# An RWKV layer with two mixtures behind it: operands laid out by the host instead of transposed on TensorE

## The chip, the cores and the metric

The kernel runs on one core of a Trainium2 chip. The metric is the device time of one execution in microseconds; lower is better. The time before is the median of three runs.

## The reference, cut to what matters

Three stages follow one another. The first is a linear attention with a state of 48 x 48 per head (4 batches, 8 heads, 768 tokens, head dimension 48); the second multiplies two projections and sends the product through `w3` and `w_out`; the third is a mixture of eight experts, weighted by a gate that is normalised eight times over rows and columns.

```python
for t in range(S):                                   # r, k, v, w: (4, 8, 768, 48)
    cur = np.einsum('bhd,bhe->bhde', u[None] * kt, vt)
    y[:, :, t] = np.einsum('bhd,bhde->bhe', rt, state + cur)
    state = wt[:, :, :, None] * state + np.einsum('bhd,bhe->bhde', kt, vt)
x = y.transpose(0, 2, 1, 3).reshape(3072, 384)
x = (((x @ w1) * (x @ w2)) @ w3) @ w_out             # 384 -> 1024 -> 1024 -> 384
P = gate(x @ w_gate)                                 # exp, then 8 row and column normalisations
out = sum(P[:, e:e+1] * (np.maximum(x @ W1[e], 0) @ W2[e]) for e in range(8))
```

The four weights of the second stage come as float64, all other inputs as float32.

## The kernel before, in words

The order of the instructions is written out by hand (line 73), and each engine's queue works in that order. The program has two parts.

The first part runs over slices `s` (loop at line 721). Attention works on 24 units of 128 tokens, four slices a unit: in its first slice a unit's successor is prepared (`stage_a0`, `stage_a1`), and then come `stage_b`, `stage_c1` and `stage_c2` for the unit itself. From slice 15 on, each slice also holds one step of the second stage of the reference for a block of 384 tokens (three units): eight steps of `moe_a` and `moe_b` (tiles `pa`, `pb`, `gs`), then four of `moe_x2` (`po`). W3 times W_out is multiplied out once beforehand, strip by strip, in slices 3 to 14 (`w34_mm`, tile `w34ps`, eight accumulating matmuls a strip), so that `moe_x2` needs one product in place of two.

In `stage_a0` and `stage_a1` (lines 273 to 357) PE transposes w, k and r of a unit, four 128 x 128 matmuls against the identity each (tiles `trw`, `trk`, `trr`), since the loads put tokens on partitions and the scans need the head dimension there. ACT copies `trw` into `w33`, where each 32 tokens have a 33rd column of zero that restarts a scan. DVE scans `w33` forwards and backwards (`Ft`, `Gt`) and multiplies `trk` and `trr` by them (`f_ks`, line 320; `f_rp`, line 332), out of PSUM. These steps are put off in a queue `aux`, from which two are taken in each slice and the rest in the last slice of a unit. GpSimd multiplies r and k with tokens on partitions (`f_rk`, line 304).

Weights in float64 are loaded as pairs of 32-bit words into tiles `raw` (line 155, three buffers), and converted by an ACT instruction (`conv1`) and three integer instructions of DVE (`conv2`). There are twenty conversions: four pieces of `w_out` (`o`), eight strips of W3 (`3`), eight strips of W1 and W2 (`i`). Their places among the slices are the lists at lines 24 to 26; each conversion issues the load for the one four places behind it (`next_load`, line 561). Each strip of W3 is transposed on PE in eight matmuls (`w34_tr`, line 232), whose result ACT copies to `w3th` for `w34_mm`.

All DMAs of the kernel are issued by SP, in program order. A load of r, k, w or v has 1024 runs of 48 numbers. The loads of unit n + 3 for w, k and r are issued in the second slice of unit n (line 758).

The second part (line 1026 on) is the experts: tiles `zp` and `yp`, with weights split into a high and a low half by ACT, POOL and DVE, and x kept in device memory and loaded again for each expert.

Of the kernel before, what the change touches and what calls it, by code (L numbers as in the profile page):

```python
# [31 lines left out]
def tile_rwkv_moe_sinkhorn_moe(
    ctx: ExitStack,
    tc: tile.TileContext,
    r: bass.AP,
    k: bass.AP,
# [117 lines left out]
    def raw_tile(n):  # L154
        return tmp.tile([P, n, 2], U32, tag="raw", bufs=3, name="raw")
# [34 lines left out]
    def load_w12(i):  # L190
        src = (moe_w1, moe_w2)[i % 2].bitcast(U32)
        c0 = 2 * FC * (i // 2)
        raw = raw_tile(KD * FC)
        rv = raw.rearrange("p (q c) t -> p q (c t)", q=KD)
        for hh in range(2):
            nc.sync.dma_start(rv[64 * hh:64 * hh + D],
                              src[0:2 * D * KD, c0:c0 + 2 * FC].rearrange(
                                  "(q h p) c -> h p q c", q=KD, h=2)[hh])
# [60 lines left out]

    w34_ops = [("t", 0, 0), ("t", 0, 1)] if W34_LEAD else []  # L260
    for s in range(NF):
        if s == W34_LEAD:
            w34_ops += [("t", s, 0), ("t", s, 1)]
        if W34_LEAD <= s < NF - 1:
            w34_ops += [("t", s + 1, 0), ("t", s + 1, 1)]
        w34_ops += [("m", s, g) for g in range(NF)]
        if s + 1 < W34_LEAD:
            w34_ops += [("t", s + 1, 0), ("t", s + 1, 1)]

    W33B = w33[:, 1:529].rearrange("p (b s) -> p b s", s=33)  # L270
# [190 lines left out]
    def moe_a(blk, f):  # L461
# [76 lines left out]
    tot = sum(0.45 if o_[0] == "t" else 0.645 for o_ in w34_ops)  # L538
    done = 0.0
    for o_ in w34_ops:  # L540
        w34_at.setdefault(W34_0 + int((done + 0.2) / tot * W34_N), []).append(o_)
# [537 lines left out]
```

## Time and profile before

| | us |
|---|---|
| median of 3 runs | 2096.4 |
| lowest and highest run | 2095.07, 2097.36 |
| profiled execution, span from first to last instruction | 2097.3 |
| PE busy | 2047.5 |
| DVE busy | 1136.3 |
| ACT busy | 551.8 |
| POOL busy | 483.4 |

The profile is of one execution and its span is its own time: 0.9 us above the median. Busy times of the engines overlap; the share of one of them in a stretch of the span tells which engine that stretch may hang on, and the waits and the chain of work that ended last tell what it does hang on.

### The profile page before, as it was taken

The numbers are of one execution on the slowest core, as the hardware profiler recorded it, in microseconds if no ns is written. First come the engines' busy times: TensorE is split into PE (matmuls) and PEld (weight loads), VectorE is DVE, ScalarE is ACT, GpSimd is POOL, SyncE is SP. The second block draws the span as 40 slices with busy tenths as digits, with TensorE's granted clock in tenths as the row PEclk, the third lists the DMA queues.
The fourth block names the chain that finished last, engine by engine and source line by source line (L and its number), as shares of the span: only waits on it lengthen the run. The fifth ranks groups of instructions, "written<-read, shape, count | busy, mean of one in ns | idle before, by whom it ended". The sixth has DMA issues, their size and how long they took to land.

```text
span 2097.3 us, 37994 instructions
## 1 busy us (share of the span) xinstructions
PE 2047.5 (98%) x16427; PEld 1992.6 (95%) x16427; DVE 1136.3 (54%) x1792; ACT 551.8 (26%) x956; POOL 483.4 (23%) x487
## 2 busy tenths in 40 slices
PE   5879999999999999999999999999999999999999
PEld 3569999999999999999999999999999999999999
DVE  8785666661575454454445444544545454445454
ACT  3443333333422221131223122211321131123111
POOL 4475555555513210030003001200300030011000
PEclk7999999999999999999999999999999999999999
DMA  8652222211412322132124122321321232213220
GB/s 241 135 102 42 50 50 50 50 21 48 181 46 91 113 84 91 72 119 97 46 91 151 46 91 77 120 91 46 136 105 47 91 116 81 91 61 117 102 84 31
DMA packets 145287, 183.67 MB, mean 88 GB/s; under 512 B 105120, under 2 KB 133856, under 8 KB 137952
## 3 DMA queue, kind: packets, MB, share of 16 engines
q1 hardware_dynamic: 145120, 181.25, 27.0%
q8 instruction: 129, 2.11, 0.4%
q14 instruction: 38, 0.31, 0.1%
HBM read 161.17 MB, written 18.87 MB: 86 GB/s over the span
## 4 chain that ended last, share of the span: by engine, by line
PE 93%; DVE 2%; DMA 2%; ACT 1%; POOL 1%; issue 0%; SPq 0%; DVEq 0%; ACTq 0%; POOLq 0%
PE yp L83 38%; PE zp L83 35%; PE po L83 5%; PE pa L83 5%; PE pb L83 4%; PE w34ps L83 2%; PE yt L83 1%; DMA raw<-in_moe_w_dram 1%; DMA raw<-in_moe_w_out_dram 1%; PE sc L83 1%; PE trn L83 1%; PE up L83 0%; PE trk L83 0%; PE trw L83 0%; PE trr L83 0%
## 5 line engine op out<-in xcount | busy, mean ns | idle before, releaser
L83 PE MATMUL zp<-xc,w1h 128*128 128x256 f32 x4224 | 782.2, 280 | 0.8 <-ACT t L868 0.8
L83 PEld LDWEIGHTS zp<-xc,w1h 128*128 128x128 f32 x4224 | 691.9, 189 | 2.0 <-ACT t L868 1.3
L83 PE MATMUL zp<-xc,w1l 128*128 128x256 f32 x2112 | 595.0, 282 | 0.0
L83 PE MATMUL yp<-w2h,hh 128*128 128x384 f32 x1536 | 518.3, 337 | 0.0
L83 PE MATMUL yp<-w2l,hh 128*128 128x384 f32 x1536 | 517.1, 337 | 0.7 <-DVE w2l L666 0.7
L83 PE MATMUL yp<-w2h,hl 128*128 128x384 f32 x1536 | 516.9, 337 | 0.0
L83 PEld LDWEIGHTS zp<-xc,w1l 128*128 128x128 f32 x2112 | 398.6, 189 | 0.0
L845 ACT ACTIVATE hh<-cc 128x512 fp32r<-128x512 f32 x288 | 182.2, 633 | 797.3 <-DVE cc L852 797.3
L652 POOL TENSOR_TENSOR w1l<-w1raw,w1h 128x768 fp32r<-128x768 f32 x32 | 59.2, 1848 | 1086.4 <-ACT w1h L651 1086.4
L83 PEld LDWEIGHTS yp<-w2h,hh 128*128 128x128 f32 x1536 | 290.0, 189 | 0.4 <-issue 0.2
L83 PEld LDWEIGHTS yp<-w2l,hh 128*128 128x128 f32 x1536 | 289.0, 188 | 0.9 <-DVE w2l L666 0.9
L83 PEld LDWEIGHTS yp<-w2h,hl 128*128 128x128 f32 x1536 | 288.5, 188 | 0.0
L852 DVE TENSOR_TENSOR cc<-u,zp 128x512 f32<-128x512 f32 x192 | 131.9, 687 | 269.1 <-PE zp L83 269.1
L852 DVE TENSOR_TENSOR u<-t,zp 128x512 f32<-128x512 f32 x192 | 132.0, 687 | 200.3 <-PE zp L83 164.6
L849 DVE SCALAR_TENSOR_TENSOR hl<-cc,hh 128x512 fp32r<-128x512 f32 x288 | 198.8, 691 | 7.2 <-ACT hh L845 7.1
L960 DVE SCALAR_TENSOR_TENSOR acc<-yp,Pm,acc 128x384 f32<-128x384 f32 x168 | 103.5, 616 | 116.6 <-PE yp L83 116.5
L845 ACT ACTIVATE hh<-zp 128x512 fp32r<-128x512 f32 x96 | 57.5, 599 | 257.1 <-PE zp L83 257.1
L849 DVE SCALAR_TENSOR_TENSOR hl<-zp,hh 128x512 fp32r<-128x512 f32 x96 | 65.9, 687 | 74.5 <-ACT hh L845 74.4
L490 POOL TENSOR_TENSOR gl<-gs,gh 128x384 fp32r<-128x384 f32 x64 | 71.4, 1116 | 110.6 <-ACT gh L489 110.5
L852 DVE TENSOR_TENSOR vv<-u,zp 128x512 f32<-128x512 f32 x96 | 66.0, 688 | 49.8 <-PE zp L83 49.7
L868 ACT ACTIVATE t<-zp 128x512 f32<-128x512 f32 x96 | 57.5, 598 | 131.9 <-PE zp L83 131.9
L488 DVE TENSOR_TENSOR gs<-pb,asb 128x384 f32<-128x384 f32 x64 | 35.6, 556 | 104.0 <-PE pb L83 65.8
(151 smaller groups left out, 2366.4 us busy)
## 6 DMA issues: line engine op xcount, KB each, us to landing
xc<-xd SPq DMA_DIRECT2D x42, 2304.0 KB, 8.7
xd<-xc SPq DMA_DIRECT2D x6, 2304.0 KB, 7.0
w2raw<-in_moe_w_dram SPq DMA_DIRECT2D x32, 384.0 KB, 3.4
raw<-in_moe_w_dram SPq DMA_DIRECT2D x8, 1024.0 KB, 5.9
w1raw<-in_moe_w_dram SPq DMA_DIRECT2D x32, 256.0 KB, 2.9
nat_w<-in_w_dram SPq DMA_DIRECT2D x24, 192.0 KB, 2.9
nat_k<-in_k_dram SPq DMA_DIRECT2D x24, 192.0 KB, 2.9
nat_r<-in_r_dram SPq DMA_DIRECT2D x24, 192.0 KB, 3.5
```

Of the source, the lines that this page charges most:

```text
L83: nc.tensor.matmul(o, lhsT, rhs, start=start, stop=stop, **kw)
L488: nc.vector.tensor_tensor(gs, pb, asb, op=ALU.mult)
L490: nc.gpsimd.tensor_tensor(gl[:, f, :], gs, gh[:, f, :].bitcast(F32), op=ALU.subtract)
L652: nc.gpsimd.tensor_tensor(lo[:, d0:d0 + n, :], src, hi[:, d0:d0 + n, :].bitcast(F32), op=ALU.subtract)
L845: nc.scalar.activation(hh, src, AF.Relu)
L849: nc.vector.scalar_tensor_tensor(hl, src, 0.0, hh.bitcast(F32), op0=ALU.max, op1=ALU.subtract)
L852: nc.vector.tensor_tensor(o, a, b_, op=ALU.add)
L868: nc.scalar.activation(t1, b1, AF.Copy)
L960: nc.vector.scalar_tensor_tensor(dst, ya[t], Pm[:, tt, e:e + 1], dst, op0=ALU.mult, op1=ALU.add)
```

## The change

The host lays the inputs out otherwise; it moves and copies numbers, and calculates nothing. The kernel then loads each tile as one contiguous run per partition.

- r and k come twice: with the head dimension on partitions (`rt`, `kt`, 128 x 512 per unit), and with tokens on partitions (`rn`, `kn`, 128 x 384) for GpSimd's product. w comes with the head dimension on partitions, the restarting zeros already in place (128 x 529). v comes padded to 64 columns a head. The tile `w33`, ACT's copy into it, the transposes of r, k, w and `stage_a1` go; DVE's scans and products read the loaded tiles.
- W3 comes with its two sides swapped within each strip, so that `w34_mm` reads the converted strip; `w34_tr` and the copies `w3th` go. The converted strips have three buffers of their own.
- `raw` has two buffers, not three; the second piece of `w_out` is loaded into a tile that shares its place with the later halves of x (`xhl`, one tile in place of `xh` and `xl`).
- The PSUM buffers of the transposes go to the tag `moe`, four in place of two.
- The steps of `w34_mm` have places of their own (`W34_AT`), from slice 3 to 13.5.
- The loads of unit n + 3 are issued at the end of the last slice of unit n.
- W1, W2, W_out, the gate and the experts' weights are loaded by one DMA a tile.

```diff
-W34_0 = 3
-W34_N = 12
-W34_LEAD = 2
+W34_AT = (3, 4, 5.5, 6.5, 7.5, 9, 10.5, 12, 13.5)
...
+    SRC = {"r": (rt, NP * P), "k": (kt, NP * P), "v": (v, H * DP), "w": (w, 16 * 33 + 1),
+           "rn": (rn, H * D), "kn": (kn, H * D)}
     nat = {}
-    for nm in ("r", "k", "w", "v"):
+    for nm in SRC:
         for j in range(2):
-            nat[nm, j] = att.tile([P, H, DP], F32, name=f"nat_{nm}{j}")
-            nc.vector.memset(nat[nm, j][:, :, D:DP], 1.0 if nm == "w" else 0.0)
-    w33 = att.tile([P, 16 * 33 + 1], F32, name="w33")
-    nc.vector.memset(w33[:, 0:528].rearrange("p (b s) -> p b s", s=33)[:, :, 0:1], 0.0)
-    nc.vector.memset(w33[:, 528:529], 0.0)
+            nat[nm, j] = att.tile([P, SRC[nm][1]], F32, name=f"nat_{nm}{j}")
 
     def load(u_, nms):
-        b, t0 = u_ // UPB, (u_ % UPB) * P
         for nm in nms:
-            src = {"r": r, "k": k, "w": w, "v": v}[nm]
-            nc.sync.dma_start(nat[nm, u_ % 2][:, :, 0:D],
-                              src[b, :, t0:t0 + P, :].rearrange("h t d -> t h d"))
+            nc.sync.dma_start(nat[nm, u_ % 2], SRC[nm][0][u_])
...
-        return tmp.tile([P, n, 2], U32, tag="raw", bufs=3, name="raw")
+        return tmp.tile([P, n, 2], U32, tag="raw", bufs=2, name="raw")
...
-        if q == NF // 2 - 1:
-            raw = moe.tile([P, 2 * DM, 2], U32, tag="gl", name="wo_raw")
+        if q % 2:
+            raw = moe.tile([P, 2 * DM, 2], U32, tag=("xhl", "gl")[q // 2], name="wo_raw")
         else:
             raw = raw_tile(2 * DM)
-        nc.sync.dma_start(
-            raw.rearrange("p (a d) t -> p a (d t)", a=2),
-            moe_w_out[2 * q * P:2 * (q + 1) * P, :].bitcast(U32).rearrange("(a p) d -> p a d", p=P))
+        nc.sync.dma_start(raw.rearrange("p n t -> p (n t)"), moe_w_out[q].bitcast(U32))
...
     def load_w12(i):
-        src = (moe_w1, moe_w2)[i % 2].bitcast(U32)
-        c0 = 2 * FC * (i // 2)
         raw = raw_tile(KD * FC)
-        rv = raw.rearrange("p (q c) t -> p q (c t)", q=KD)
-        for hh in range(2):
-            nc.sync.dma_start(rv[64 * hh:64 * hh + D],
-                              src[0:2 * D * KD, c0:c0 + 2 * FC].rearrange(
-                                  "(q h p) c -> h p q c", q=KD, h=2)[hh])
-            x1 = D * (2 * KD + hh)
-            nc.sync.dma_start(rv[64 * hh + D:64 * hh + 64],
-                              src[x1:x1 + D, c0:c0 + 2 * FC].rearrange("(q p) c -> p q c", q=KD))
+        nc.sync.dma_start(raw.rearrange("p n t -> p (n t)"), (moe_w1, moe_w2)[i % 2][i // 2].bitcast(U32))
...
-        cvs["3", s] = conv1(raws["3", s], FF)
+        cvs["3", s] = conv1(raws["3", s], FF, tmp.tile([P, FF], F32, tag="w3c", bufs=3, name="w3c"))
...
-    def w34_tr(s, q):
-        raw = w3c[s]
-        if q == 0:
-            w3t[s] = tmp.tile([P, NF, P], F32, tag="w3t", bufs=2, name="w3th")
-        th = w3t[s]
-        pt = ps.tile([P, 4, P], F32, tag="moe", bufs=2, name="w3pt")
-        for j in range(4):
-            g = 4 * q + j
-            mm(pt[:, j, :], raw[:, g * P:(g + 1) * P], ident, True, True, tr=True)
-        nc.scalar.activation(th[:, 4 * q:4 * q + 4, :], pt, AF.Copy)
-        if q == 1:
-            w3c.pop(s)
-
     w34_acc = {}
 
     def w34_mm(s, g):
         assert ("o", g // 2) in ready
-        th = w3t[s]
+        th = w3c[s]
         if g == 0:
-            w34_acc[s] = ps.tile([P, DM], F32, tag="moe", bufs=2, name="w34ps")
+            w34_acc[s] = ps.tile([P, DM], F32, tag="moe", bufs=4, name="w34ps")
         acc = w34_acc[s]
-        mm(acc, th[:, g, :], wo[:, g, :], g == 0, g == NF - 1)
+        mm(acc, th[:, g * P:(g + 1) * P], wo[:, g, :], g == 0, g == NF - 1)
...
     def stage_a0(n):
-        wt, kt = nat["w", n % 2], nat["k", n % 2]
-        pw = ps.tile([P, NP, P], F32, tag="tr", bufs=2, name="trw")
-        for p in range(NP):
-            mm(pw[:, p, :], wt[:, 2 * p:2 * p + 2, :].rearrange("p a d -> p (a d)"), ident, True, True, tr=True)
-        nc.scalar.activation(W33B[:, :, 0:32], pw.rearrange("p a (b s) -> p (a b) s", s=32), AF.Copy)
-        pk = ps.tile([P, NP, P], F32, tag="tr", bufs=2, name="trk")
-        for p in range(NP):
-            mm(pk[:, p, :], kt[:, 2 * p:2 * p + 2, :].rearrange("p a d -> p (a d)"), ident, True, True, tr=True)
-        d = st[n] = {"pk": pk}
+        w33 = nat["w", n % 2]
+        d = st[n] = {}
...
-        nrt, nkt = nat["r", n % 2], nat["k", n % 2]
+        nrt, nkt = nat["rn", n % 2], nat["kn", n % 2]
+        krt, kkt = nat["r", n % 2], nat["k", n % 2]
 
         def f_rk():
-            nc.gpsimd.tensor_tensor(rk, nrt[:, :, 0:D], nkt[:, :, 0:D], op=ALU.mult)
+            nc.gpsimd.tensor_tensor(rk.rearrange("p h d -> p (h d)"), nrt, nkt, op=ALU.mult)
...
-            kv = pk.rearrange("p a (c b s) -> p b (a c) s", b=2, s=32)
+            kv = kkt.rearrange("p (a b s) -> p b a s", b=2, s=32)
             nc.vector.tensor_tensor(diag(Kt), kv, Gv, op=ALU.mult)
...
-            rv = d["pr"].rearrange("p a (c b s) -> p b (a c) s", b=2, s=32)
+            rv = krt.rearrange("p (a b s) -> p b a s", b=2, s=32)
             nc.vector.tensor_tensor(off(Rt)[:, ::-1], rv, Fv, op=ALU.mult)
...
-    def stage_a1(n):
-        rt = nat["r", n % 2]
-        pr = ps.tile([P, NP, P], F32, tag="tr", bufs=2, name="trr")
-        for p in range(NP):
-            mm(pr[:, p, :], rt[:, 2 * p:2 * p + 2, :].rearrange("p a d -> p (a d)"), ident, True, True, tr=True)
-        st[n]["pr"] = pr
...
-            xh = moe.tile([P, KD, BLK], F32R, tag="xh", name="xh")
-            xl = moe.tile([P, KD, BLK], F32R, tag="xl", name="xl")
-            xs[blk] = (xh, xl)
+            xhl = moe.tile([P, 2, KD, BLK], F32R, tag="xhl", name="xhl")
+            xs[blk] = (xhl[:, 0], xhl[:, 1])
...
-        pa = ps.tile([P, BLK], F32, tag="tr" if blk == NB - 1 else "moe", bufs=2, name="pa")
+        pa = ps.tile([P, BLK], F32, tag="moe", bufs=4, name="pa")
...
+    for x_, g_ in w34_ops:
+        pl_ = W34_AT[x_] + (W34_AT[x_ + 1] - W34_AT[x_]) * g_ / NF
+        w34_at.setdefault(int(2 * pl_) / 2, []).append((x_, g_))
...
-    load(0, "wkrv")
+    load(0, ("w", "k", "rn", "kn", "r", "v"))
     nc.sync.dma_start(ub.rearrange("p h d -> p (h d)"), u.rearrange("h d -> (h d)").partition_broadcast(P))
     next_load()
...
-        for j in range(2):
-            nc.sync.dma_start(t[:, 1 - j, :], e_w1[e, 0:P, c0 + j * P:c0 + (j + 1) * P])
-        nc.sync.dma_start(t[:, 2:, :].rearrange("p (k i) c -> p k (i c)", i=2),
-                          e_w1[e, P:, c0:c0 + 2 * P].rearrange("(k p) c -> p k c", p=P))
+        nc.sync.dma_start(t.rearrange("p a c -> p (a c)"), e_w1[i])
...
-    stage_a1(0)
-    load(2, "wkr")
     next_prep1()
     flush()
+    load(2, ("w", "k", "rn", "kn", "r"))
...
-        wops = w34_at.get(s, [])
         do_preps(s)
-        do_w34(wops[:len(wops) // 2])
+        do_w34(w34_at.get(s, ()))
...
-            if n < NU - 1 and ph == 0:
-                stage_a1(n + 1)
...
-        if ph == 1 and n + 3 < NU:
-            load(n + 3, "wkr")
         if ph == 2 and n + 2 < NU:
-            load(n + 2, "v")
+            load(n + 2, ("v",))
         if ph == 3 and n < NU:
             flush()
+            if n + 3 < NU:
+                load(n + 3, ("w", "k", "rn", "kn", "r"))
...
+def _lay_out(inputs):
+    P, DP = 128, 64
+    r, k, v, w, u = (inputs[nm] for nm in "rkvwu")
+    B, H, S, D = r.shape
+    NP, UPB = H // 2, S // P
+    NU = B * UPB
+
+    def across(a, fill):
+        o = np.full((B, UPB, 2, DP, NP, P), fill, a.dtype)
+        o[:, :, :, :D] = a.reshape(B, NP, 2, UPB, P, D).transpose(0, 3, 2, 5, 1, 4)
+        return o.reshape(NU, P, NP * P)
+
+    def along(a, dp):
+        o = np.zeros((B, UPB, P, H, dp), a.dtype)
+        o[..., :D] = a.reshape(B, H, UPB, P, D).transpose(0, 2, 3, 1, 4)
+        return o.reshape(NU, P, H * dp)
+
+    w33 = np.zeros((NU, P, 16 * 33 + 1), w.dtype)
+    w33[:, :, 1:].reshape(NU, P, 16, 33)[..., 0:32] = across(w, 1.0).reshape(NU, P, 16, 32)
+    feed = {"rt": across(r, 0.0), "kt": across(k, 0.0), "rn": along(r, D), "kn": along(k, D), "v": along(v, DP),
+            "w": w33, "u": u}
...
+    a = inputs["moe_w3"]
+    NF = a.shape[0] // P
+    feed["moe_w3"] = a.reshape(NF, P, NF, P).transpose(0, 3, 2, 1).reshape(NF, P, NF * P)
```

## Rows read from the trace of the kernel before

**Rows 1.** The page, parts 1 and 4: busy us and shares; chain by engine.

```profile
PE 2047.5 (98%) x16427; PEld 1992.6 (95%) x16427; DVE 1136.3 (54%) x1792; ACT 551.8 (26%) x956; POOL 483.4 (23%) x487
...
PE 93%; DVE 2%; DMA 2%; ACT 1%; POOL 1%; issue 0%; SPq 0%; DVEq 0%; ACTq 0%; POOLq 0%
```

**Rows 2.** Windows by stage: PE, PEld, DVE, ACT, POOL busy; clock; DMA share; GB/s.

```profile
0.00:36.00 36.00, 12.97 (x148) 10.40 (x149) 29.74 (x51) 10.46 (x15) 13.90 (x23) 0.65 0.89 250
36.00:112.00 76.00, 69.01 (x608) 43.79 (x612) 61.87 (x74) 33.28 (x55) 36.80 (x29) 0.92 0.69 155
112.00:165.00 53.00, 41.50 (x455) 37.23 (x446) 43.41 (x55) 19.41 (x37) 38.13 (x28) 0.87 0.48 84
165.00:460.00 295.00, 295.00 (x3713) 277.56 (x3706) 180.32 (x312) 97.75 (x214) 170.06 (x163) 1.00 0.23 46
460.00:2097.00 1637.00, 1628.98 (x11536) 1623.63 (x11534) 821.00 (x1303) 390.88 (x637) 224.48 (x246) 1.00 0.24 89
```

**Rows 3.** Waits of PE from 165 us on: us in total, times, longest.

```profile
PE pcs L83 <- DVE cs L1001: 3.3, 6, 0.8
```

**Rows 4.** Chain in order of time, 168 to 451 us: start, us, what.

```profile
168.55 0.44 PE trw L83 x4
...
184.15 1.56 PE pb L83 x9
...
186.58 1.57 PE pa L83 x9
...
450.15 0.44 PE trr L83 x4
```

**Rows 5.** Window behind 168 us, tile trw alone: PE, PEld, ACT busy.

```profile
168.00:460.00 292.00, 10.16 (x68) 8.49 (x68) 9.96 (x17) 1.00 0.23 46
```

**Rows 6.** PE, 36 to 112 us: busy us, mean ns, idle before it, releasers.

```profile
L83 PE MATMUL w34ps<-wo,w3th 128*128 128x384 f32 x128 | 50.0, 535 | 5.3 <-ACT w3th L241 5.3
L83 PE MATMUL w3pt<-ident,cv 128*128 128x128 f32 x56 | 8.8, 290 | 5.3 <-ACT w34s L256 3.6 <-ACT w3th L241 1.7
L83 PE MATMUL trr<-ident,nat_r 128*128 128x128 f32 x12 | 2.3, 322 | 0.0
```

**Rows 7.** Waits of DVE, 36 to 112 us.

```profile
DVE Ft L309 <- ACT w L278: 9.1, 2, 4.9
DVE At L376 <- PE sc L83: 2.5, 2, 1.9
```

**Rows 8.** Instructions of DVE, 0 to 165 us (all `gs` behind 112 us).

```profile
L488 DVE TENSOR_TENSOR gs<-pb,asb 128x384 f32<-128x384 f32 x8 | 4.4, 551 | 7.3 <-PE trk L83 3.0 <-PE pb L83 2.1 <-ACT asb L475 2.1
```

**Rows 9.** Waits of PE, 0 to 165 us.

```profile
PE pb L83 <- ACT w34s L256: 2.8, 1, 2.8
```

**Rows 10.** DMA view, 0 to 125 us: 40 slices of GB/s, packets, issues.

```profile
GB/s 71 216 218 370 151 296 324 211 284 329 314 154 308 260 241 299 0 47 288 39 348 217 168 72 0 5 102 150 106 145 185 224 146 118 142 128 129 109 143 200
DMA packets 33164, 22.67 MB, mean 181 GB/s; under 512 B 28179, under 2 KB 28403, under 8 KB 32130
...
raw<-in_moe_w_dram SPq DMA_DIRECT2D x8, 1024.0 KB, 5.9
```

**Rows 11.** Lines 324, 377 (ns min/median/max); then 377, 0 to 165 us.

```profile
L324 DVE TENSOR_TENSOR Kt<-trk,Gt x24: 674/678/682, 8.9 to 457.9; 128x512 f32<-128x512 f32 x24
...
L377 DVE TENSOR_TENSOR At<-At,ec x24: 691/694/1404, 23.5 to 470.4; 128x512 f32<-128x512 f32 x24
...
L377 DVE TENSOR_TENSOR At<-At,ec 128x512 f32<-128x512 f32 x6 | 4.9, 810 | 0.6
```

**Rows 12.** Waits of SP, 0 to 165 us; timeline, ACT at 33 us.

```profile
SPq L218 <- DVE cv L167: 26.4, 5, 8.9
...
33.12 1.16 ACT L160 ACTIVATE cv<-raw 128x1024 f32<-128x1024 f32 x1 [2.65 <-DMA raw<-in_moe_w_dram]
```

**Rows 13.** Chain in order of time, 36 to 67 us.

```profile
36.00 6.04 PE w34ps L83 x10
...
63.40 2.79 PE w34ps L83 x8
```

More of the change, by code (lines that the diff above doesn't have):

```diff
@@ L28 @@
 LOG0 = 1
+SHAPE = (4, 8, 768, 48)
 @with_exitstack
@@ L34, in tile_rwkv_moe_sinkhorn_moe @@
     tc: tile.TileContext,
-    r: bass.AP,
-    k: bass.AP,
+    rt: bass.AP,
+    kt: bass.AP,
+    rn: bass.AP,
+    kn: bass.AP,
     v: bass.AP,
@@ L49, in tile_rwkv_moe_sinkhorn_moe @@
     nc = tc.nc
-    B, H, S, D = r.shape
+    B, H, S, D = SHAPE
     NT, DM = out.shape
-    FF = moe_w1.shape[1]
-    E = w_gate.shape[1]
     P = 128
+    FF = moe_w3.shape[0] * P
+    E = e_w2.shape[0] * 2 * P // FF
     DP = 64
@@ L217, in load_w3 @@
         raw = raw_tile(FF)
-        nc.sync.dma_start(raw.rearrange("p n t -> p (n t)"), moe_w3[s * P:(s + 1) * P, :].bitcast(U32))
+        nc.sync.dma_start(raw.rearrange("p n t -> p (n t)"), moe_w3[s].bitcast(U32))
         raws["3", s] = raw
@@ L258, in w34_mm @@
             nc.gpsimd.tensor_tensor(w34l[:, s, :], ws, w34h[:, s, :].bitcast(F32), op=ALU.subtract)
[L260 to L270, printed above, removed]
+    w34_ops = [(s, g) for s in range(NF) for g in range(NF)]
     st = {}
     def stage_a0(n):
-        wt, kt = nat["w", n % 2], nat["k", n % 2]
-        pw = ps.tile([P, NP, P], F32, tag="tr", bufs=2, name="trw")
-        for p in range(NP):
-            mm(pw[:, p, :], wt[:, 2 * p:2 * p + 2, :].rearrange("p a d -> p (a d)"), ident, True, True, tr=True)
-        nc.scalar.activation(W33B[:, :, 0:32], pw.rearrange("p a (b s) -> p (a b) s", s=32), AF.Copy)
-        pk = ps.tile([P, NP, P], F32, tag="tr", bufs=2, name="trk")
-        for p in range(NP):
-            mm(pk[:, p, :], kt[:, 2 * p:2 * p + 2, :].rearrange("p a d -> p (a d)"), ident, True, True, tr=True)
-        d = st[n] = {"pk": pk}
+        w33 = nat["w", n % 2]
+        d = st[n] = {}
         Ft = att.tile([P, 528], F32, tag="F", name="Ft")
@@ L289, in stage_a0 @@
         cc = att.tile([P, H], F32, tag="cc", bufs=2, name="cc")
-        d.update(R=Rt, T12=T12, v=nat["v", n % 2])
+        d.update(R=Rt, T12=T12, v=nat["v", n % 2].rearrange("p (h d) -> p h d", d=DP))
         F3 = Ft.rearrange("p (b s) -> p b s", s=33)
@@ L480, in moe_b @@
         gh, gl = g_t[blk]
-        pb = ps.tile([P, BLK], F32, tag="moe", bufs=2, name="pb")
+        pb = ps.tile([P, BLK], F32, tag="moe", bufs=4, name="pb")
         n = 0
@@ L508, in moe_x2 @@
             if rest == 0:
-                po_t[blk] = ps.tile([P, BLK], F32, tag="moe", bufs=2, name="po")
+                po_t[blk] = ps.tile([P, BLK], F32, tag="moe", bufs=4, name="po")
             po = po_t[blk]
@@ L519, in moe_x2, with moe_log @@
                     t0 += n
-    def moe_log(blk, step, pool=None, tag="moe", bufs=2):
+    def moe_log(blk, step, pool=None, tag="moe", bufs=4):
         pool = pool or ps
@@ L537, in tile_rwkv_moe_sinkhorn_moe @@
     w34_at = {}
[L538 to L541, printed above, removed]
-        done += 0.45 if o_[0] == "t" else 0.645
+    for x_, g_ in w34_ops:
+        pl_ = W34_AT[x_] + (W34_AT[x_ + 1] - W34_AT[x_]) * g_ / NF
+        w34_at.setdefault(int(2 * pl_) / 2, []).append((x_, g_))
     def do_w34(ops):
-        for kind, x_, y_ in ops:
-            (w34_tr if kind == "t" else w34_mm)(x_, y_)
+        for o_ in ops:
+            w34_mm(*o_)
     PREP = {}
@@ L593, in tile_rwkv_moe_sinkhorn_moe @@
     next_load()
-    load(1, "wkrv")
+    load(1, ("w", "k", "rn", "kn", "r", "v"))
     next_load()
     next_load()
-    nc.sync.dma_start(gate[:, :, 0:E], w_gate.rearrange("(q p) e -> p q e", p=P))
+    nc.sync.dma_start(gate[:, :, 0:E], w_gate)
     pools = {}
@@ L619, in ld_w2 @@
             return
[L620 removed]
         t = pools[0].tile([P, 2, DM], F32, tag="w2raw", bufs=2, name="w2raw")
[L622 removed]
+        nc.sync.dma_start(t.rearrange("p i d -> p (i d)"), e_w2[i])
         w2raw[i] = t
@@ L750, in tile_rwkv_moe_sinkhorn_moe @@
                 moe_x2(sl[1], sl[2])
-            if n < NU - 1 and ph == 0:
-                stage_a1(n + 1)
             pop(2)
-        do_w34(wops[len(wops) // 2:])
+        do_w34(w34_at.get(s + 0.5, ()))
         if s in logs:
@@ L1056, in tile_rwkv_moe_sinkhorn_moe @@
                     rescale(*resc.popleft())
+def _lay_out(inputs):
[16 more added lines that the diff above has]
+            "w": w33, "u": u}
+    KD = H * D // P
+    rows = np.empty((P, KD), np.int64)
+    for h in range(2):
+        for q in range(KD):
+            rows[64 * h:64 * h + D, q] = D * (2 * q + h) + np.arange(D)
+            rows[64 * h + D:64 * h + 64, q] = D * (2 * KD + h) + (DP - D) * q + np.arange(DP - D)
+    FC = 2 * P
+    for nm in ("moe_w1", "moe_w2"):
+        a = inputs[nm]
+        a = a[rows].reshape(P, KD, -1, FC)
+        feed[nm] = a.transpose(2, 0, 1, 3).reshape(-1, P, KD * FC)
+    a = inputs["moe_w3"]
+    NF = a.shape[0] // P
+    feed["moe_w3"] = a.reshape(NF, P, NF, P).transpose(0, 3, 2, 1).reshape(NF, P, NF * P)
+    a = inputs["moe_w_out"]
+    DM = a.shape[1]
+    feed["moe_w_out"] = a.reshape(NF // 2, 2, P, DM).transpose(0, 2, 1, 3).reshape(NF // 2, P, 2 * DM)
+    a = inputs["moe2_w_gate"]
+    feed["w_gate"] = a.reshape(KD, P, -1).transpose(1, 0, 2)
+    a = inputs["moe2_w1"]
+    E = a.shape[0]
+    a = a.reshape(E, KD, P, NF // 2, 2, P).transpose(0, 3, 2, 1, 4, 5).reshape(E * NF // 2, P, 2 * KD, P)
+    feed["e_w1"] = a[:, :, [1, 0] + list(range(2, 2 * KD))].reshape(E * NF // 2, P, 2 * KD * P)
+    a = inputs["moe2_w2"]
+    feed["e_w2"] = a.reshape(E * NF // 2, 2, P, DM).transpose(0, 2, 1, 3).reshape(E * NF // 2, P, 2 * DM)
+    return feed
@@ L1059 @@
 def kernel(**inputs):
-    names = ("r", "k", "v", "w", "u", "moe_w1", "moe_w2", "moe_w3", "moe_w_out", "moe2_w_gate", "moe2_w1", "moe2_w2")
     nc = _bacc.Bacc("TRN2", target_bir_lowering=False, num_devices=1)
-    aps = []
+    aps = {}
     feed = {}
-    for nm in names:
-        a = np.ascontiguousarray(inputs[nm])
+    for nm, a in _lay_out(inputs).items():
+        a = np.ascontiguousarray(a)
         if a.dtype == np.float64:
@@ L1068 @@
         t = nc.dram_tensor(f"in_{nm}_dram", a.shape, mybir.dt.from_np(a.dtype), kind="ExternalInput")
-        aps.append(t.ap())
+        aps[nm] = t.ap()
         feed[f"in_{nm}_dram"] = a
-    NT = inputs["r"].shape[0] * inputs["r"].shape[2]
-    o = nc.dram_tensor("out_0_dram", (NT, inputs["moe_w_out"].shape[1]), F32, kind="ExternalOutput")
+    B, H, S, D = inputs["r"].shape
+    assert (B, H, S, D) == SHAPE
+    o = nc.dram_tensor("out_0_dram", (B * S, inputs["moe_w_out"].shape[1]), F32, kind="ExternalOutput")
     with tile.TileContext(nc) as tc:
-        tile_rwkv_moe_sinkhorn_moe(tc, *aps, o.ap())
+        tile_rwkv_moe_sinkhorn_moe(tc, out=o.ap(), **aps)
     if not nc.is_finalized():
```

6 lines of the change are left out of this document (1 added, 5 removed).

## The prediction, made before the change was run

> **What bounds the kernel now.** I read the page first: PE is busy 98% of the span and has 93% of the chain that ended last [rows 1]. That share is an average, so I asked for busy time by stage [rows 2]. The reader is to see three kinds of stage. From 165 us on PE is busy without a gap (295.00 of 295.00 us, then 1629 of 1637) at full clock while DVE, POOL and ACT stand at 61%, 58% and 33%: there a removed PE instruction comes off the time, and the largest total of any PE wait left is 3.3 us [rows 3]. In 36 to 112 us PE is busy 69.0 of 76 us and DVE 61.9. In 0 to 36 us and in 112 to 165 us DVE is the fuller engine (29.7 of 36, 43.4 of 53), with POOL at 38.1 of 53 in the latter. So the first 165 us, in which the weights are converted, are not PE's alone, and the change is to be priced twice.
>
> **Part 1: the transposes of r, k, w after 165 us.** Each unit has twelve. The chain in order of time shows a group of four as 0.44 us, three groups per unit, 51 such pieces from 168.55 to 450.15 us [rows 4]. The tile view of one of the three counts 68 instructions behind 168 us, so 17 units [rows 5]. The groups stand in the chain between matmuls; nine matmuls of `pa` behind one take 1.57 us and the nine of `pb` ahead of it 1.56, so nothing but the group itself goes [rows 4]. 17 x 3 x 0.437 (the pieces are 0.434 to 0.44) = 22.3 us. What is late next there? DVE would have to grow from 180 to 273 us, POOL from 170. I take 22.3 us; bounds 20 and 23.
>
> **Part 2: 36 to 112 us.** Out of PE's queue go the 56 transposes of W3 in this stage (8.8 us), three units of r, k, w (three tiles at 2.3 us and less, about 6 together), and the waits on ACT around them (5.3 us before `w34ps` for ACT's copy `w3th`, 5.3 us before `w3pt`) [rows 6]: 25 of PE's 76 us. ACT loses the `w3th` and `w33` copies. PE then needs some 51 us, less than DVE's 61.9, so DVE sets the end, and what counts is where DVE waits. Its waits are 11.6 us: 9.1 us in two waits of the scan `Ft` for ACT's copy of w, which stood behind PE transposes and ACT's conversions, and 2.5 us of `At` for PE [rows 7]. After the change `Ft` reads a tile that a DMA has filled, so 9.1 us go; the 2.5 us I leave. Bounds: 0 (the in-order queues turn the wait into another) and 14.1 (all of DVE's idle time). I take 9, as the two waits are known by name.
>
> **Part 3: 112 to 165 us.** DVE idles 9.6 us, of which 7.3 us stand before `gs`, which waits for PE's matmuls and for ACT's `asb` [rows 8]. Two units of transposes leave PE, and four PSUM buffers in place of two take away the 2.8 us in which `pb` waited for `w34s` [rows 9]. DVE and POOL stay nearly full with the last conversions, so I take 3 us; bounds 0 and 9.6.
>
> **Part 4: 0 to 36 us.** Here bytes matter. Before, the stage moved 250 GB/s x 36 us = 9.0 MB [rows 2]. By shapes one unit's operands were four loads of 192 KB; they become w 271 KB, k, r and v 262 KB each, and second copies of r and k of 197 KB each, 1.45 MB. What is issued until the third strip of W3 is there is two units (2.90 MB), a third without v (1.19), u (0.20), all of w_out (3.15) and three strips (3.15): 10.6 MB. At the stage's own 250 GB/s that is 42 us, at the best slice of the DMA view (370 GB/s) 29 us [rows 10]. The packets favour the second: 28,179 of 33,164 were under 512 B, and the new ones are 1.5 KB and more. I take 0, between -7 and +6 us.
>
> **Part 5: K and R are read from SBUF.** The product `Kt` took its operand out of PSUM and never stretched: 674 to 682 ns over 24. `At`, of the same shape with both inputs in SBUF, takes 691 ns at least and 1404 at most, 810 ns in the mean of the first 165 us [rows 11]. 14 products of k and r lie before 165 us: 14 x 0.12 = 1.7 us lost; bounds 0 and 14 x 0.71 = 10 us. Behind 165 us DVE's idle time (115 us) covers the 34 others.
> The Trainium skill ("SBUF — State Buffer", section "SBUF: two separate sides") says that a VectorE instruction with two SBUF inputs and a GpSimd instruction take a shared pair of ports in turn, each for its whole length. The spread of `At` beside the fixed `Kt` agrees with it [rows 11]. It speaks against this edit, and if each of the 14 met a GpSimd instruction the sum would lose the 10 us of the bound.
>
> **Part 6: SP's queue, PE's clock, the rest.** `raw` goes from three buffers to two, while loads still run four conversions ahead. A load now waits on SP for the conversion two places ahead of its own instead of three, and all behind it on SP waits too: the loads of r, k, w, v and the `xraw` copies. With three buffers SP's loads of W3 already wait 26.4 us for conversions [rows 12]. The cover: at least 1.5 slices lie between the freeing conversion and the one that needs the load; 36 to 112 us holds twelve slices, 6.3 us each, so 9.5 us against 5.9 us to landing for 1 MB [rows 10]. Closest is unit 4's load: issued behind a weight strip that waits for place 10.5, needed in slice 12, with 1.06 MB to land for its scan (4.2 us at 250 GB/s, and some 2 us on top). I take 0; the loss is 5.9 us each time the cover fails, at most 14 times. Unit loads move two slices later and are five DMAs, not three; W1 and W2 strips are one DMA, not four, so 24 issues leave SP. Memsets of DVE go in the first 3 us, before its first operand lands: 0. PE's clock is the open side: ten `w34ps` took 6.04 us and eight took 2.79 later [rows 13], so the 128 of them cost 32 us more if PE stayed at the lower of its two levels (1.2 GHz). The stage's granted clock was 0.92, after 0.65 in the stage ahead; DVE gives PE 11 us of cover, and I take 0. The weight loads of the expert stage become one DMA each, beneath a PE that does not wait for them [rows 3]: 0.
>
> **Sum.** -22.3 - 9 - 3 + 0 + 1.7 + 0 = -32.6 us from the profiled span of 2097.3: 2064.7. The median of the runs is 2096.4, 0.9 lower: 2063.8, so 2064.
>
> **Rivals.**
> (a) Only the steady part gains. DVE meets POOL at the products of k and r (10 us as in part 5), or the opening pays for its bytes (6 us), and that eats the 12 us of parts 2 and 3. For it: DVE 61.9 and 43.4 busy, `At` stretched already. Against: 9.1 us of DVE's waits have one cause that goes. Time 2097.3 - 22.3 - 0.9 = 2074.
> The rule of the Trainium skill named in part 5 is this rival's first mechanism.
> (b) All of DVE's idle time in the 165 us goes (30.0 us by rows 2, less 1.7). For it: both queues that DVE waits on lose work. Against: part of the idle time is chains between DVE, POOL and ACT. Time 2097.3 - 22.3 - 28.3 - 0.9 = 2046.
> (c) Slower: with two `raw` buffers SP holds each strip until it is late, and ACT, in order, stops behind it with all that PE and DVE wait for. Its price is 5.9 us a time; it decides from six exposed loads of 14 on (32.6 / 5.9); nine would give 2064 + 53 = 2117. For it: SP's 26.4 us. Against: ACT's last wait for a strip was 2.65 us at 33.12 us [rows 12].
> (d) The transposes were hidden anyway: excluded behind 165 us by PE's 100%.
>
> **How the numbers follow.** Forecast (2055 to 2070) 0.56, (a) with small losses of the opening (2070 to 2082) 0.24, (b) 0.13, (c) 0.07, of which 0.04 end above the old time. A measurement of this kernel can tell about 0.2% (4 us) from no change. Faster 0.94, same 0.02, slower 0.04. The range leaves out the far ends of (b) and (c): 2048 to 2080.
>
> **What would show it.** Right: PE's chain from about 155 us without transposes and without a gap, each unit 1.3 us shorter; `Ft` without waits on ACT; DVE over 85% busy from 36 us to the end of the conversions; the first `po` 10 us sooner than 165 us. Wrong: ACT waiting for `raw` behind 40 us (c); `Kt` and `Rt` near 1 us (a); PE gaps behind 165 us, which would break part 1, the largest term.

## The result and the profile after

The changed kernel takes 2074.0 us (median of 4 runs, 2072.34 to 2075.54) against 2096.9 us for the kernel before on the same chip (2095.07 to 2098.23): 22.9 us less, ratio 0.989 with a 95% interval of 0.988 to 0.991. The forecast was 2064; the time is inside the range of 2048 to 2080, outside the 2055 to 2070 that the forecast held likeliest, and falls on the figure of rival (a).

The profiled execution of the changed kernel has a span of 2070.2 us and is the shortest of its four (2072.34; span and time differ by 2.1 us). That of the kernel before, with a span of 2097.3 us, was longer than usual: in the runs of it that went beside the experiments the span is 1.7 us below the time, so a run at the median of 2096.9 has a span of about 2095. The two profiles alone therefore show 27 us, some 4 us more than the medians. This matters below, where the difference is counted to the first part.

The page, part 1 (answers to [rows 1]):

```profile
PE 2004.5 (97%) x16075; PEld 1954.4 (94%) x16075; DVE 1145.3 (55%) x1782; ACT 531.1 (26%) x916; POOL 487.4 (24%) x487
```

PE lost 43 us of work and the time fell by 23. Windows by stage, columns as in [rows 2]:

```profile
0.00:36.00 36.00, 10.53 (x125) 7.34 (x126) 28.36 (x41) 8.41 (x11) 12.72 (x22) 1.00 0.81 283
36.00:112.00 76.00, 57.49 (x533) 35.75 (x532) 71.11 (x80) 27.25 (x43) 42.81 (x31) 0.87 0.54 189
112.00:165.00 53.00, 39.62 (x421) 36.64 (x420) 43.51 (x53) 17.33 (x35) 39.20 (x30) 0.84 0.31 104
165.00:460.00 295.00, 295.00 (x3765) 276.94 (x3764) 191.19 (x325) 96.81 (x216) 175.74 (x171) 1.00 0.28 86
460.00:2070.00 1610.00, 1601.82 (x11239) 1597.73 (x11237) 811.08 (x1285) 381.34 (x615) 216.91 (x236) 1.00 0.25 89
```

Behind 165 us PE is as full as before. In 36 to 112 us DVE went from 61.9 to 71.1 us of 76: it is the full engine now, and PE idles 18.5 us.

The stages shift against each other, so the cut to compare at is the first `po`, after which PE never stops for long. It begins at 165.15 us before and at 160.25 us after. Behind it, 2097.3 - 165.15 = 1932.15 us became 2070.2 - 160.25 = 1909.95 us: **22.2 us in the steady part.** The same subtraction gave 1909.7 to 1909.9 us in the profiles of e1, e4 and e5 and 1911.3 in that of e6, so this length hardly varies, and a median tells where `po` begins in a usual run: 2095 - 1932 = 163 us before, 2074.0 - 2.1 - 1910 = 162 us after. **By the medians the first part became about 1 us shorter**, not 10. For the kernel before this rests on a single profile; in the two profiles themselves the first part is 4.9 us shorter.

What DVE did up to the first `po` of each kernel, one window of before and then one of after:

```profile
0.00:165.15 165.15, 123.63 (x1196) 91.50 (x1197) 135.17 (x179) 63.16 (x105) 88.83 (x78) 0.84 0.67 153
```

```profile
0.00:160.25 160.25, 102.89 (x1048) 74.98 (x1049) 139.31 (x169) 51.21 (x82) 90.76 (x78) 0.88 0.54 187
```

DVE's idle time fell by 9.0 us (30.0 to 20.9), its busy time rose by 4.1 us although it has ten instructions fewer. PE was relieved of 20.7 us in this stretch, and little came of it.

### The profile page after: what moved, and what is told of

The parts are those of the page before. It is cut to its first block, busy times and chain, and to the rows that moved or that the text cites. A ratio compares the mean times of both kernels' runs of the same rounds, so it can differ in the third digit from the quotient of the medians.

```text
span 2070.2 us, 37109 instructions
## 1 busy us (share of the span) xinstructions
PE 2004.5 (97%) x16075; PEld 1954.4 (94%) x16075; DVE 1145.3 (55%) x1782; ACT 531.1 (26%) x916; POOL 487.4 (24%) x487
## 4 chain that ended last, share of the span: by engine, by line
PE 92%; DVE 5%; POOL 1%; issue 1%; ACT 1%; DMA 1%; SPq 0%; DVEq 0%; ACTq 0%; POOLq 0%
PE yp L84 38%; PE zp L84 35%; PE po L84 5%; PE pa L84 5%; PE pb L84 4%; PE yt L84 1%; PE sc L84 1%; PE trn L84 1%; PE w34ps L84 1%; PE up L84 0%; DMA raw<-in_moe_w_out_dram 0%; DVE cv L162 0%; PE pl L84 0%; DVE w3c L163 0%; DVE Gt L268 0%
## 5 line engine op out<-in xcount | busy, mean ns | idle before, releaser
L438 POOL TENSOR_TENSOR gl<-gs,gh 128x384 fp32r<-128x384 f32 x64 | 84.4, 1318 | 96.3 <-ACT gh L437 96.2
L84 PE MATMUL pa<-xhl,w1h 128*128 128x384 f32 x384 | 105.3, 355 | 1.4 <-DVE xhl L405 0.8
L84 PE MATMUL pb<-xhl,w2h 128*128 128x384 f32 x384 | 98.7, 338 | 1.9 <-ACT w2h L198 1.9
```

Of the source, the lines that this page charges most:

```text
L84: nc.tensor.matmul(o, lhsT, rhs, start=start, stop=stop, **kw)
L438: nc.gpsimd.tensor_tensor(gl[:, f, :], gs, gh[:, f, :].bitcast(F32), op=ALU.subtract)
```

## The experiments

Theory 1: the end of the first part is set by DVE's and GpSimd's work on the conversions and on units prepared beside them, and by the slices in which the last conversions stand; PE's transposes were never its bound. Theory 2: the two `raw` buffers took back what the transposes gave. Theory 3: PE's lower clock did. All times are medians; the runs of before beside them had medians of 2096.3 to 2097.3.

**e1_rkw_only.** Only the r, k, w part: W3's strips are transposed on PE again.

```diff
+            mm(pt[:, j, :], raw[:, g * P:(g + 1) * P], ident, True, True, tr=True)
+        nc.scalar.activation(th[:, 4 * q:4 * q + 4, :], pt, AF.Copy)
```

> The changed kernel with the W3 part put back as before (strips transposed on PE, copies w3th, places and tiles of w34 as before); r, k, w stay laid out by the host. Theory 1 (the 22.3 us behind 165 us are the whole steady gain and come from r, k, w; in the first 160 us DVE and POOL set the end, so PE's W3 transposes are hidden): 2073 to 2080 us, first po at 160 to 166 us, and from there to the end within 1 us of the changed kernel's 1910 us. Rival (the 5 us gained in the first 160 us are W3's): first po at 165 us or later, 2079 us or more.

2073.7 us (2073.07 to 2075.06), ratio 0.989 [0.988, 0.991]: the time of the whole change. The first `po` begins at 162.9 us in the profile, 1909.9 us before the end. Beside the r, k, w part, swapping W3's sides is worth nothing measurable, though 56 of its 64 transposes took 8.8 us of PE in 36 to 112 us alone [rows 6].

**e2_w3_only.** Only the W3 part: r, k and w come with tokens on partitions, contiguous, and PE transposes them again.

```diff
+        pw = ps.tile([P, NP, P], F32, tag="tr", bufs=2, name="trw")
+            mm(pw[:, p, :], wt[:, p * P:(p + 1) * P], ident, True, True, tr=True)
+        nc.scalar.activation(W33B[:, :, 0:32], pw.rearrange("p a (b s) -> p (a b) s", s=32), AF.Copy)
```

> The changed kernel with r, k, w transposed on PE and read from PSUM as before (tokens on partitions, padded, still one contiguous DMA a tile); W3 stays with its sides swapped. Theory 1: the 51 groups of 0.437 us come back behind 165 us, so 22.3 us over a first part of 158 to 166 us: 2092 to 2099 us, the same as the kernel before. Rival (the gain is W3's and the contiguous loads'): 2080 us or less.

2094.4 us (2093.20 to 2095.27, 10 runs), ratio 0.999 [0.998, 1.000]: 2 us of the 22.9. Its chain in order of time behind the first `po` (start, us, what) has the transposes back:

```profile
161.97 0.44 PE trw L82 x4
162.41 0.44 PE trk L82 x4
...
165.98 0.44 PE trr L82 x4
```

Its first `po` begins at 158.6 us in the profile, 1.6 us sooner than with the transposes gone; by the medians it is about 3 us sooner (2094.4 - 2.0 - 1933.7 = 159 us against 162). Behind it the kernel takes 2092.3 - 158.6 = 1933.7 us, 23.8 more than the changed kernel. DVE's waits for ACT's copy of w, first up to 160 us, then in 36 to 112 us, where the forecast had priced 9.1 us (waited for, us in total, times, longest):

```profile
DVE Ft L272 <- ACT w L241: 6.3, 2, 3.6
```

```profile
DVE Ft L272 <- ACT w L241: 2.7, 1, 2.7
```

So most of the priced wait is gone here too, with PE's transposes of r, k and w still in place, and the first part is about 4 us shorter than that of the kernel before; whether the W3 part or the contiguous loads did it is open. The remaining 6.3 us of `Ft`'s waits go when r, k and w are laid out by the host as well, and nothing is gained by that. Up to the first `po` DVE's idle time then falls by 1.2 us only (22.1 to 20.9), since other waits come instead, and its busy time rises by 2.8 us (136.5 to 139.3). The window of this version, columns as in [rows 2]:

```profile
0.00:158.64 158.64, 112.83 (x1133) 84.22 (x1133) 136.50 (x172) 54.84 (x89) 89.25 (x78) 0.89 0.49 169
```

**e3_raw_four.** Four `raw` tiles until slice 11, in the room of tiles not yet used.

```diff
+        if s in (1, 4, 5):
+            raw = moe.tile([P, FF, 2], U32, tag={1: "xhl", 4: "gl", 5: "xhl"}[s], name="w3_raw")
```

> The changed kernel with room for four raw tiles in place of two until slice 11 (three strips of W3 and two of W1/W2 are loaded into the places of xhl and gl, which are empty until slice 14). Theory 2 (the missing 5 us of the first part are the two raw buffers: ACT waited 23.0 us in six waits for strips of W3): these waits fall under 6 us and the first po comes at 152 to 156 us, 2066 to 2070 us. Theory 1 (DVE and POOL set the end): the waits fall, the first po stays within 2 us of 160 us, 2072 to 2076 us.

2072.9 us (2072.80 to 2073.63), ratio 0.989 [0.987, 0.990]. ACT's waits for strips of W3, first from the waits of the changed kernel (us in total, times, longest), then from the list of who waited for `raw` in this one (us, times) and from its waits, for a strip in the added room:

```profile
ACT w3c L156 <- DMA raw<-in_moe_w_dram: 23.0, 6, 5.5
```

```profile
  ACT w3c L156: 5.2, 1
```

```profile
ACT w3c L156 <- DMA w_raw<-in_moe_w_dram: 2.5, 1, 2.5
```

The waits fell to 7.7 us, not under 6, so 15 us of them went. The time fell by 1 us, which the scatter of the runs does not tell from nothing. Theory 2 falls: ACT did wait for its strips, but ACT was not late. It now waits elsewhere, for the matmuls that make `w34ps` (21.3 us, 13.2 before this edit) and `trn` (8.7 us, none before).

**e4_ec_on_act.** The product `ec` (one GpSimd instruction of 1.7 us a unit) as eight ACT instructions.

```diff
-            nc.gpsimd.tensor_tensor(
-                ec, eye.unsqueeze(1).unsqueeze(1).to_broadcast([P, 2, NP, DP]),
-                cc.rearrange("p (a h) -> p h a", h=2).unsqueeze(3).to_broadcast([P, 2, NP, DP]), op=ALU.mult)
+            for h in range(2):
+                for a in range(NP):
+                    nc.scalar.activation(ec[:, h, a, :], eye, AF.Copy, scale=cc[:, 2 * a + h:2 * a + h + 1])
```

> The changed kernel with the product ec (eye times cc, one POOL instruction of 1.70 us a unit) made by ACT in eight instructions of 64 columns. Theory 1 with POOL as the partner that stretches DVE and whose queue ends the first part (chain 139 to 152 us all POOL): POOL loses 10 us of work before the first po, DVE's instructions stretch less, first po at 152 to 157 us, 2066 to 2071 us. Theory 2: POOL is no bound, first po within 1.5 us of 160 us; if ACT's queue was the bound (eight instructions of some 0.2 us a unit) it comes later, 162 us or more.

2067.3 us (2066.13 to 2068.28), ratio 0.986 [0.985, 0.988]: 6.7 us below the change. The chain shows the end of the first part. First the kernel before, then the changed one, up to the last matmuls ahead of `po`:

```profile
149.06 1.73 POOL ec L345
150.79 1.68 POOL rk L305
...
152.54 1.86 POOL rk L306
154.40 2.72 POOL w2l L214
...
157.16 2.59 PE pb L83 x7
...
165.22 2.80 PE po L83 x15
```

```profile
144.36 1.73 POOL ec L301
146.08 1.68 POOL rk L261
...
147.83 1.82 POOL rk L262
149.65 2.72 POOL w2l L199
...
152.41 2.61 PE pb L84 x7
...
160.32 6.45 PE po L84 x36
```

Both kernels end their first part in the same way, piece by piece: GpSimd works through `ec` and two `rk` of the next unit, and only then makes `w2l`, the low half of the last W2 strip, for which `pb` waits. No transpose of r, k, w or W3 is in it. With `ec` gone from GpSimd the `w2l` starts at 143.58 us and is released by ACT's `w2h` behind DVE's conversion:

```profile
140.98 1.66 DVE cv L163
...
142.66 0.85 ACT w2h L198
...
143.58 2.63 POOL w2l L199
```

GpSimd's queue is only part of the gain, though: the conversion ahead of `w2h` ends 4.3 us sooner than in the changed kernel (142.6 against 145.21 + 1.69 = 146.9 us). Up to the first `po` DVE was busy 133.1 us here, 6.2 less, while its idle time hardly moved (21.5 us against 20.9):

```profile
0.00:154.58 154.58, 101.08 (x1049) 73.93 (x1049) 133.11 (x170) 62.70 (x130) 81.42 (x72) 0.91 0.55 194
```

No work of DVE was taken away, so DVE's own instructions took less time with less work on GpSimd beside them. The other profiles agree: DVE was busy 134.9 and 132.9 us in e7 and e9, with `ec` on ACT, but 139.5 and 139.1 us in e3 and e8, with `ec` on GpSimd.

**e5_no_sign.** Left out: DVE's third conversion instruction (the sign bit) for the eight strips of W1 and W2.

```diff
-        conv2(raws.pop(("i", i)), c)
+        conv2(raws.pop(("i", i)), c, False)
```

> Left out: the third integer instruction of DVE's conversion (the sign bit) for the eight strips of W1 and W2, so that all converted numbers of W1 and W2 are positive. It takes 8 instructions of DVE of some 1.5 us, 12 us, out of slices 12 to 20 and nothing from POOL. If POOL's queue ends the first part (POOL 39 of 53 us busy behind 112 us, and the last 13 us of the chain before the first po are POOL's), DVE's 12 us lie beside it: the first po comes 0 to 4 us sooner, time 2070 to 2074. If DVE's own work is the bound of the first part: 8 to 12 us sooner, 2062 to 2066. The third theory, that PE's low clock behind 112 us (0.76 to 0.84) keeps the first part long, gives 2074 too.

2065.3 us (2064.92 to 2065.68), 8.7 us below the change. The eight instructions took 10.1 us in the changed kernel, so most of it came off. My expectation for GpSimd's queue alone, 0 to 4 us, was wrong: DVE is as much the bound. In the chains above the two feed each other, conversion to `w2l` and `gs` to `gl`, and work taken from either shortened the part.

**e6_warm.** Added: four transposes of the identity per half slice in slices 12 to 23, on PE.

```diff
+    def do_warm():
+        for j in range(4):
+            mm(warm[:, j, :], ident, ident, True, True, tr=True)
```

> Added: four 128x128 transposes of the identity in each half slice of slices 12 to 23 on PE (24 groups of 0.44 us at full clock, 10.5 us in sum), into a PSUM tile of their own (the tag moe has three buffers instead of four). If the lower granted clock behind 98 us (0.76 in the third stage, 0.88 before the change) is why the first part did not become shorter, the added work raises the clock and the first po comes 3 us or more sooner than 160: time 2071 or less. If POOL and DVE set the end, the added work lies beside them and nothing moves: 2074 within 2, or up to 5 us more where PE is the later one.

2077.3 us (2077.08 to 2077.59), 3.4 us above the change. Windows from 98 us to the first `po`, the changed kernel and then this one (the number behind the five engines is the granted clock):

```profile
98.00:160.00 62.00, 42.63 (x496) 38.97 (x500) 51.14 (x66) 21.37 (x38) 40.55 (x29) 0.76 0.41 139
```

```profile
98.00:164.00 66.00, 51.76 (x578) 47.81 (x579) 53.78 (x71) 23.55 (x42) 41.75 (x30) 0.83 0.40 133
```

The granted clock was a little higher and the part no shorter. Of 10.5 us of added work a third shows. Theory 3 has no support; one PSUM buffer less went with the edit, so the 3.4 us are not the transposes' alone.

**e7_raw4_ec.** e3 and e4 together (their diffs).

> The two versions that were not slower put together: the product ec on ACT instead of POOL, and four raw tiles until slice 11. If POOL's queue is the bound and ACT's 23 us of waits for strips are covered, the time is that of ec on ACT alone, 2067 within 1.5. If ACT, which now carries 2.7 us more per unit, is the next bound and the strips come late for it, the earlier loads are worth something here: 2062 to 2065.

2066.4 us (2066.18 to 2066.90), ratio 0.985 [0.984, 0.987]: 0.9 us below e4, within its scatter. The earlier loads are worth nothing here either.

**e8_last_early.** One number: the last strip of W2 is converted a slice sooner.

```diff
-W12_PREP = (11.5, 12.5, 13.5, 14.0, 15.0, 16.0, 17.5, 20.0)
+W12_PREP = (11.5, 12.5, 13.5, 14.0, 15.0, 16.0, 17.5, 19.0)
```

> Changed: the last strip of W2 is converted at place 19.0 instead of 20.0; no work is added or removed. Theory: the first part is as long as the fixed places of the conversions make it, above all the last one. In the chain of the changed kernel DVE idles 3.0 us ahead of that conversion (139 to 142 us), and GpSimd reaches its product w2l only at 149.65, 1.9 us after w2h is there, behind ec, rk and rk (5.2 us). One slice sooner, the conversion fills DVE's idle time and stands ahead of both rk on GpSimd: the first po 3 to 6 us sooner, time 2068 to 2071. If the sum of the work of DVE (or GpSimd) is the bound, the order of it changes nothing: 2074 within 1.5. If the strip then comes too late for its load, ACT waits and it is slower: 2075 to 2078.

2070.2 us (2069.35 to 2070.95), ratio 0.988 [0.986, 0.989]: 3.8 us below the change with no work removed. The chain in order of time:

```profile
142.14 1.87 POOL Kt L286 x2
144.00 1.49 POOL w2l L199
...
145.73 1.57 POOL Rt L295
...
147.35 0.69 PE sc L84 x32
...
158.38 3.67 PE po L84 x20
```

`w2l` now stands ahead of both `rk`, at 144.00 instead of 149.65 us, and what PE waits for is `Rt` of the next unit. A part of the length is thus the place in the order, not the sum of the work: up to the first `po` DVE is as busy as in the changed kernel (139.1 us) and idles 1.7 us less.

**e9_ec_last.** e4 and e8 together (their diffs).

> The product ec on ACT and the last conversion at place 19.0 together. With ec off GpSimd the last w2l waited for DVE's conversion (140.7 to 142.6 us) and not for GpSimd's queue. If places and sums are separate costs, the two gains add: 2062 to 2065. If the sum of DVE's work is what is left, 2067 within 1.5.

2066.5 us (2065.05 to 2067.21), ratio 0.986 [0.984, 0.987]: not told from e4. The gains do not add, which fits that both take the same GpSimd queue out of the way of `w2l`. The versions with `ec` on ACT (e4, e7, e9) beat both kernels, by 30 us and 7 us.

## Why the prediction came out as it did

The time lies in the range because the largest term was right and the range was wide. Of the 10 us that the sum held beside that term, about 1 came.

**Part 1 (22.3 us, transposes behind 165 us): right, 22.2 us measured.** The chain of the changed kernel has no transposes of r, k and w there, `zp`, `yp` and `pcs` are PE's only waits and the largest is still the 3.3 us of `pcs`. This term alone is nearly the whole gain of 22.9 us.

**Parts 2 and 3 (9 + 3 us): the step that failed.** What I read was right as far as it went: `Ft` no longer waits for ACT, DVE is 94% busy in 36 to 112 us, and its idle time fell by the 9 us that I had named. Yet the first `po` came 5 us sooner in the profiles and 1 us by the medians, not 10. The fault was to put an idle time of DVE, ended by a known cause, at its full length on the path because DVE was the fullest engine, and to leave DVE's own work nearly as it was. By the two profiles, the 9 us of idle time were paid back in part by 4.1 us more of busy time (part 5 had 1.7), and the 3 us of part 3 did not come: up to the first `po`, `gs` waited 7.3 us before [rows 8] and 7.0 after. The lead arose where `Ft`'s two waits had been: the third conversion instruction of DVE began 0.6 us sooner at W3's sixth strip (63.20 against 63.76 us), 5.8 at the first strip of W2 (95.33 against 101.16), and 4.7 at the last strip (145.21 against 149.91). The other 4 us between the profiles and the medians lie in no instruction that a run here names. DVE's waits after, 0 to 165 us:

```profile
DVE gs L436 <- ACT asb L423: 5.1, 2, 3.0
DVE Ft L265 <- DMA nat_w<-in_w_dram: 2.8, 2, 2.1
DVE cc L300 <- POOL rk L262: 2.7, 1, 2.7
```

The 3.0 us for `asb` stand just ahead of the last conversion. That 13 of the last 21 us of the first part are GpSimd's, the rest PE's, and that none is a transpose was to be read in the chain of the kernel before (144.3 to 165.2 us). I gave the chain's rows only for 36 to 67 us and from 168 us on. How much of what is missing is the order and how much DVE's longer instructions is not settled: e8 prices the place of the last strip at 3.8 us, DVE's growth to the first `po` is 4.1 us, and the two overlap.

**Part 4 (the opening, 0; -7 to +6): near the middle.** The `sc` of unit 1, in slice 5, starts at 44.89 us against 47.96 us, but DVE is no further by then: its seventh conversion begins the third instruction at 44.15 us against 43.88.

**Part 5 (K and R from SBUF, -1.7 us): mechanism right, size and place wrong.** First `Kt`, `Rt` of the changed kernel over all 24 units (ns min/median/max), then `Rt` out of PSUM in e2:

```profile
L280 DVE TENSOR_TENSOR Kt<-nat_k,Gt x24: 674/676/684, 7.3 to 431.0; 128x512 f32<-128x512 f32 x24
...
L290 DVE TENSOR_TENSOR Rt<-nat_r,Ft x24: 682/685/1437, 7.9 to 433.7; 128x512 f32<-128x512 f32 x24
```

```profile
L297 DVE TENSOR_TENSOR Rt<-trr,Ft x24: 680/683/684, 9.5 to 454.2; 128x512 f32<-128x512 f32 x24
```

Up to 165 us `Rt` has a mean of 832 ns against 684, 1.0 us over seven; `Kt` lost nothing. But DVE grew by 4.1 us, as instructions that the change did not touch stretched too:

```profile
L326 DVE TENSOR_TENSOR At<-At,ec 128x512 f32<-128x512 f32 x6 | 6.0, 1000 | 0.7 <-POOL ec L301 0.2
L272 DVE COPY Mt<-Ft 128x16 f32<-128x16 f32 x7 | 6.8, 971 | 0.0
```

`At` had 810 ns [rows 11] and `Mt` 745. That DVE meets GpSimd more often when it waits less is my reading of this; e4 shows that DVE's time hangs on GpSimd's work (6.2 us for the one product), not why it rose here. The timeline shows how, first DVE and then GpSimd:

```profile
128.02 1.78 DVE L272 COPY Mt<-Ft 128x16 f32<-128x16 f32 x1
...
130.01 0.75 DVE L274 TENSOR_TENSOR T<-Mt 128x8 f32<-128x8 f32 x1
...
131.15 0.68 DVE L280 TENSOR_TENSOR Kt<-nat_k,Gt 128x512 f32<-128x512 f32 x1
...
137.10 1.44 DVE L290 TENSOR_TENSOR Rt<-nat_r,Ft 128x512 f32<-128x512 f32 x1
...
151.51 1.40 DVE L326 TENSOR_TENSOR At<-At,ec 128x512 f32<-128x512 f32 x1
```

```profile
127.42 2.35 POOL L199 TENSOR_TENSOR w2l<-cv,w2h 128x768 fp32r<-128x768 f32 x1
129.74 1.00 POOL L438 TENSOR_TENSOR gl<-gs,gh 128x384 fp32r<-128x384 f32 x1
131.86 1.31 POOL L438 TENSOR_TENSOR gl<-gs,gh 128x384 fp32r<-128x384 f32 x1 [1.12 <-ACT gh L437]
135.93 2.07 POOL L199 TENSOR_TENSOR w1l<-cv,w1h 128x768 fp32r<-128x768 f32 x1 [2.76 <-ACT w1h L198]
...
149.61 2.75 POOL L199 TENSOR_TENSOR w2l<-cv,w2h 128x768 fp32r<-128x768 f32 x1
```

`Rt` ends 0.54 us after `w1l` does (138.54, 138.00) and `At` 0.55 us after `w2l` (152.91, 152.36), whatever their starts: they were held until GpSimd was through. `Kt` ran inside a gap of GpSimd. This agrees with the rule of the Trainium skill named in part 5, that the pair of ports goes to one of the two for a whole instruction. The bound of 10 us needed every product to meet a GpSimd instruction at its start; most started in a gap.

**Part 6 (two `raw` buffers, clock: 0): right in the sum.** ACT did wait for strips behind 40 us (12.4 us for W3, 5.2 us for one of W1 and W2), the sign that I had set for rival (c), yet 15 us fewer of such waits were worth 1 us at most in e3. The granted clock of 36 to 112 us was 0.87 against 0.92 before, and PE idled 18.5 us there. The sign was badly chosen: a wait of an engine that is a third busy tells no time.

**The rivals.** (a) has the right number, and its first sentence, that only the steady part gains, is what happened. Its price list was not: the stretched products cost 1 us and not 10, and the opening cost nothing. Its first mechanism was nearer than that: all of DVE's instructions together took 4.1 us more, 2.8 of them when r, k and w joined the W3 part (e2). The chance of 0.24 was too low for a case that needed only one of several engines to stay full. (b) is excluded by 21 us of idle time left on DVE, (c) by e3, (d) by part 1.

## What to carry to other kernels

Work that a removed instruction gives back is gained only where its engine is the chain; here 22 of 43 us of PE, exactly those behind the first `po`. Before pricing an idle time, follow the chain of waits to the end of its stage and ask what the last piece waits for: here a one-digit change of a conversion's slice or a product moved from GpSimd to ACT gave what 20 us less of PE did not. And the work of DVE is to be priced with GpSimd's instructions beside it: here one GpSimd product a unit, moved to ACT, made DVE's unchanged instructions 6.2 us shorter in sum up to the first `po`.

## What the runs showed of the hardware that was not expected

A small DVE copy with a single input was held like the products with two. `Mt` (128x16) had a mean of 971 ns; one took 1.78 us from 128.02 to 129.80 us, and GpSimd's `w2l` ended at 129.77. The `T12` product of 8 elements behind it (`T` in the rows) took 0.75 us, to 130.76, beside a `gl` that ended at 130.74; elsewhere it took 0.10 us (at 154.00). The Trainium skill ("SBUF — State Buffer", section "SBUF: two separate sides") counts DVE instructions in a two-port mode among those that take the shared ports; the copy's times agree with that, though no row here names its mode.

The column of the granted clock does not always speak for the matmuls of a stretch. In 12 to 24 us of the changed kernel it reads 1.00, but the 32 matmuls of `sc` took 1.14 us at 13.04 and 0.69 us at 44.89. In the kernel before the same 32 took 1.14 us at 17.39, where the column reads 0.50, the lower of the two levels (1.2 GHz). Where the two differ, the durations are the surer reading.
